# Starting the sums of x beside the last pieces of the attention's stage, with TensorE pinned to the source's order and two lent slots

## The chip, the cores and the metric

One core of a Trainium2 chip. The metric is the device time of one execution in microseconds; the kernel before takes 644.06 us (median of 3 runs, 642.32 to 644.40).

## What is computed

```python
# q, k, v: (2, 8, 768, 64) f32; sink of 4 keys, window of 128
a = softmax(where(is_sink | in_window, q @ k.T / 8, -1e9))
x = (a @ v) as 1536 rows of 512
x = ((x @ w_a) * (x @ w_b)) @ w_out            # 512 -> 1536 -> 512, first net
h = max(x @ moe2_w_in, 0)
out = (h * h) @ moe2_w_out                     # 512 -> 2048 -> 512, second net
```

Weights arrive in double precision, two 32-bit words a number.

## The kernel before

Every matmul is in single precision worked out of two rounded halves: a tile t becomes `hi` (a cast on ScalarE) and `lo = t - hi` (a subtraction on VectorE); the helper `split` does both (L66, L67). A product is then three matmuls: hi by hi, hi by lo, lo by hi. In the rows the halves of weights are `wh` and `wl`, those of x `xh` and `xl`, those of an intermediate g `gh` and `gl`. x is kept transposed in three blocks of 512 rows.

**Attention's stage.** A loop over 24 groups and three steps more (`attention_fast`), all engines in the source's order (`manual_schedule(engines=ORDERED)`). Beside it run *pieces* of the first net: of four columns blocks of w_a and w_b, for each of the three blocks of x, 12 matmuls into the PSUM tile `psa` (L657). There are 24 pieces, made by `Ffn.ahead`; `beside.asked` counts the pieces asked for in the loop. A piece of w_a is emptied by ScalarE into `u` (L670), the one of w_b by VectorE into `gs` (L674). `psa` has two buffers, so a piece waits for the emptying of the one two before it. The pieces of the third block need the last rows of x and so run after the loop, in `for at in beside.work` of `run`. There no engine's order is fixed: the planner of the framework orders what the source issues, by its own estimate of times. `ahead` yields None after each emptying; each such None calls `F.beat()`.

**Beats.** `beat` takes one step of a list of `chores` and lets `W.ahead()` convert one tile of weights every third beat (`PACE = 3`), if a slot (`W.free`) is there. A conversion of a weight tile (`Weights.stages`) is one ScalarE operation, four on VectorE (L534 to L541), a cast and a subtraction (L546, L548). `W.done` gives slots back when their weights are used up.

**The sums of x.** From phase 2 on, two blocks are multiplied by a scheme with seven products in place of eight (`unit`); it needs sums of the quarters of x in blocks 0 and 1. `first_sums` makes them in two halves (k = 0, 1), each in ten steps: four adds that put xh and xl together again into tiles `ks` (L704), two steps of two subtractions each (`sums_of`, L686 to L690), four splits, of which one overwrites block 1 of xh and xl. Each of these VectorE instructions is passed to `keep_in_program_order`, which puts it behind the instruction of its engine issued just before it in the source. So 20 steps in 20 beats.

**The second part** (`Ffn.run`), TensorE alone in the source's order. First the product with w_out of the eager columns: `one` for block 1, `two` for block 2, `held` for block 0, matmuls into `acc` (L916), each g split into gh and gl (3 buffers each, from a pool `wk` that is opened after the attention's pools have been closed), 6 matmuls for each half of g and a beat after each: 8, 8 and 4 beats. The first g is split into a lent slot of weights in place of gh and gl, so its matmuls read `wh` and `wl`. Then phase 2 with its first `unit` (px, py, pz, L786).

Of the kernel before, what the change touches and what calls it, by code (L numbers as in the profile page):

```python
# [21 lines left out]
AHEAD1 = 4  # L22
# [23 lines left out]
ET = mybir.EngineType  # L46
# [17 lines left out]
def split(nc, hi, lo, src, lo_eng=None):  # L64

    nc.scalar.copy(hi, src)  # L66
    return (lo_eng or nc.vector).tensor_sub(lo, src, hi.bitcast(F32))  # L67
# [571 lines left out]
class Ffn:  # L639
# [317 lines left out]
    def run(self, ps_y, ps_a, wk, keep):  # L957

        W = self.W
        self.ps_a, self.wk, self.keep = ps_a, wk, keep  # L960
        self.fresh, self.uses, self.fill, self.later, self.half = set(), {}, [], [], set()
        n1 = AHEAD1
        sizes = [len(p) for p in W.phases]

        def acc(ph, blk, ps, groups, final=0):
            return dict(net=ph >= W.second, blk=blk, ps=[], pool=(ps, "aaaa" if ps is ps_y else "xyzz"), total=3 * groups,
                        at=[0] * 4, final=final)

        def gs_of(blk):
            return [(1, f, self.gs[blk][:, f]) for f in range(n1)]  # L970

        one = acc(1, 1, ps_y, n1)
        slot = W.free.pop(0)
        split(self.tc.nc, *slot, gs_of(1)[0][2])
        self.chores.append(self.first_sums())
        yield from self.rest(one, gs_of(1), ready=[slot])
        W.free.append(slot)
        self.drain(one)
        two = acc(1, 2, ps_a, n1)
        yield from self.rest(two, gs_of(2))  # L980
        self.drain(two)
        held = acc(1, 0, ps_y, n1 + sizes[2])
        yield from self.rest(held, gs_of(0), 2)
        plan = {2: (0, 2, 1), 3: (1, 0, 2), W.second: (0, 1, 2)}
        for ph in range(W.second + 1, len(sizes)):
            a, b, c = plan[ph - 1]
            plan[ph] = (c, a, b)
        for ph in range(2, len(sizes)):
            now, mid, end = plan[ph]
            self.ph, self.now = ph, now  # L990
            self.kept = {mid: [], end: []}
            n, both = sizes[ph], ph < W.second
            lastly = ph in (W.second - 1, len(sizes) - 1)
            final = 2 - both if lastly else 0
            while self.chore():
                pass
            self.acc = held
            for key in self.later:
                self.queue(*key[:3], self.halves(key[3]))
            self.later = []  # L1000
            if ph == W.second:
                self.fill.append((self.drain, (held,)))
                self.acc = acc(ph, now, ps_y, n)
            self.acc["final"] = final
            late = LATE if both and lastly else 0
            step = 1 if both else 2
            other = acc(ph, mid, ps_a, n, final)
            lag, early = [], []

            def items(blk):  # L1010
                return [(ph, f, g) for f, g in sorted(self.kept[blk], key=lambda x: x[0])]

            def hook():
                if f + step == n:
                    early.append(self.halves(items(mid)[0][2]))

            for f in range(0, n, step):
                if f < n - late:
                    lag.append(f)
                woven = None  # L1020
                if lag and (lag[0] < f or ph != W.second):
                    woven = self.plain(ph, lag.pop(0))
                yield from self.unit(ph, f, woven, hook)
            for f in lag:
                for it in self.plain(ph, f):
                    yield from it
            while self.fill and not (both and now == 1 and len(self.fill) < 3) and len(self.fill) > 2 * (step - 1):
                self.more()
                yield
            yield from self.rest(other, items(mid)[:1], ready=early)  # L1030
            while self.fill:
                self.more()
                yield
            self.drain(self.acc)
            yield from self.rest(other, items(mid)[1:])
            self.drain(other)
            if not lastly:
                held = acc(ph, end, ps_y, n + sizes[ph + 1])
                yield from self.rest(held, items(end), 2)
                continue  # L1040
            held = acc(ph, end, ps_y, n, final)
            if both:
                self.chores.append(self.second_sums())
                self.pace = 2
                for f in range(n - late, n):
                    for it in self.plain(ph, f):
                        yield from it
                yield from self.rest(held, items(end), 2)
                continue
            yield from self.rest(held, items(end)[:-2])  # L1050
            its = items(end)[-2:]
            gs = [self.halves(g) for _, _, g in its]
            for d in range(4):
                for (p_, f, _), g in zip(its, gs):
                    self.outer(held, p_, f, g, 0, range(d, d + 1))
                self.drain(held, d)
            yield


@with_exitstack  # L1060
def sliding_window_moe_kernel(ctx, tc, q, k, v, vs, span, w_a, w_b, w_out, w_in2, w_out2, out):
    nc = tc.nc
    NT, DM = out.shape
    cp = ctx.enter_context(tc.tile_pool(name="cp", bufs=1))
    xp = ctx.enter_context(tc.tile_pool(name="xp", bufs=1))
    xh = xp.tile([P, DM // P, NT], F32R, name="xh")
    xl = xp.tile([P, DM // P, NT], F32R, name="xl")
    rp = ctx.enter_context(tc.tile_pool(name="rp", bufs=3))
    sa = ctx.enter_context(tc.tile_pool(name="sa", bufs=1))

    def slots(pool, n):
        return [(pool.tile([P, 512], F32R, name=f"wh{j}"), pool.tile([P, 512], F32R, name=f"wl{j}")) for j in range(n)]

    first = slots(sa, FIRST)
    zero = cp.tile([P, P], mybir.dt.bfloat16, name="zero")
    nc.vector.memset(zero, 0.0)
    mk = ctx.enter_context(ExitStack())
    tp = mk.enter_context(tc.tile_pool(name="mk", bufs=1, side="right"))
    c = setup(tc, cp, tp, span)

    def run(attend):
        W = Weights(tc, cp, rp, w_a, w_b, w_out, w_in2, w_out2)
        W.free = list(first)
        F = Ffn(tc, W, xh, xl, xp, out)
        with ExitStack() as c0:
            c0.callback(mk.close)
            wk0 = c0.enter_context(tc.tile_pool(name="wk0", bufs=2, side="right"))
            beside = Beside(tc, W, F, wk0, c0, zero, NT)
            with ExitStack() as c1, tc.manual_schedule(engines=ORDERED):
                attend(c1, beside)  # L1090
            with tc.tile_pool(name="sb", bufs=1) as sb, tc.tile_pool(name="ks", bufs=NKEEP) as keep:
                sx = slots(sb, NSUM)
                F.sx = {(n, k): sx[3 * k + n - 2] for n in range(2, 5) for k in range(2)}
                F.keep = keep
                for at in beside.work:
                    if at is None:
                        F.beat()
                c0.close()
                with ExitStack() as c2:
                    ps_y = c2.enter_context(tc.tile_pool(name="ps_y", bufs=4, space=PSUM))  # L1100
                    ps_a = c2.enter_context(tc.tile_pool(name="ps_a", bufs=1, space=PSUM))
                    wk = c2.enter_context(tc.tile_pool(name="wk", bufs=2))
                    c2.enter_context(tc.manual_schedule(engines={ET.PE}))
                    for _ in F.run(ps_y, ps_a, wk, keep):
                        F.beat()

    def attend_any(ctx, beside):
        attention_any(tc, c, q, k, v, xh, xl)
        beside.open()

    run(lambda ctx, beside: attention_fast(tc, ctx, c, cp, tp, q, k, v, vs, xh, xl, beside))
    slow = nc.values_load(c.slow[0:1, 0:1], min_val=0, max_val=1,
                          skip_runtime_bounds_check_because="the flag is 0 or 1")
    with tc.If(slow != 0):
        run(attend_any)
# [68 lines left out]
```

## Time and the profile before

| | |
|---|---|
| runs | 642.32, 644.06, 644.40 us; median 644.06 |
| profiled execution | 644.62 us |
| its span (first to last instruction) | 642.8 us |
| mean granted TensorE clock | 0.996 |
| TensorE busy | 621.2 us, 97% |
| VectorE busy | 483.1 us, 75% |
| ScalarE busy | 309.6 us, 48% |

The span is one execution on the chip, engine by engine: PE is TensorE's matmuls, DVE VectorE, ACT ScalarE. Times in the rows are microseconds from the span's start. A granted clock of 1.00 is TensorE's full clock.

### The profile page before, as it was taken

The page shows a single profiled execution, that of the slowest core. Times are in us where ns is not written, and L with a number is a line of the kernel's source. Part 1 is how long each engine was busy: PE and PEld are TensorE (multiplying, and loading weights), DVE is VectorE, ACT ScalarE, POOL GpSimd, SP SyncE. Part 2 cuts the span into 40 slices and gives each one's busy share as a digit, 9 for nine tenths or more (in the row PEclk, how much of TensorE's full clock was granted, in tenths as well). Part 3 has the DMA queues.
Part 4 walks back from the last instruction along what each step waited for, and adds up shares of the span by engine and source line. Part 5 has one row for each costly group of instructions (what it writes and reads, how often), then busy time and mean ns, then how long its engine had stood idle before and what let it go on. Part 6 is the DMA issues. An engine that isn't in the chain of part 4 may idle for free.

```text
span 642.8 us, 8846 instructions
## 1 busy us (share of the span) xinstructions
PE 621.2 (97%) x3110; PEld 498.0 (77%) x3110; DVE 483.1 (75%) x1094; ACT 309.6 (48%) x706; POOL 56.2 (9%) x132
## 2 busy tenths in 40 slices
PE   9889999998989999999999999999999999999996
PEld 6557777786767888888877787888887888888884
DVE  6989988246998867867858999986697769844352
ACT  6888777413664334523434645555435344322220
POOL 2564254300000000000000000000000000000000
PEclk9999999999998999999999999999999999999999
DMA  8634422012213230132212112232132112000023
GB/s 276 215 123 134 166 83 96 3 33 65 66 66 110 87 99 34 65 99 65 67 65 67 33 34 65 72 126 70 61 98 66 60 39 65 1 1 2 1 90 111
DMA packets 17413, 49.48 MB, mean 77 GB/s; under 512 B 2064, under 2 KB 2576, under 8 KB 17360
## 3 DMA queue, kind: packets, MB, share of 16 engines
q1 hardware_dynamic: 17216, 48.83, 23.4%
q8 instruction: 26, 0.43, 0.3%
q14 instruction: 27, 0.22, 0.1%
q10 hardware_dynamic: 144, 0.00, 0.0%
HBM read 45.68 MB, written 3.15 MB: 76 GB/s over the span
## 4 chain that ended last, share of the span: by engine, by line
PE 66%; DVE 8%; issue 1%; ACT 0%; DVEq 0%
PE acc L916 31%; PE psa L657 14%; PE px L786 12%; PE py L786 6%; PE pz L786 3%; DVE gl L67 1%; DVE wtmp L538 1%; DVE part L936 1%; DVE wtmp L534 1%; DVE wl L67 1%; DVE wtmp L541 1%; DVE wl L548 1%; DVE ks L704 0%; DVE xl L67 0%; ACT wtmp L530 0%
## 5 line engine op out<-in xcount | busy, mean ns | idle before, releaser
L657 PE MATMUL psa<-xh,wh 128*128 128x512 f32 x224 | 88.8, 396 | 0.5 <-DVE part L936 0.5
L657 PE MATMUL psa<-xh,wl 128*128 128x512 f32 x224 | 87.4, 390 | 0.0
L657 PE MATMUL psa<-xl,wh 128*128 128x512 f32 x224 | 87.2, 389 | 0.0
L916 PE MATMUL acc<-wh,gl 128*128 128x512 f32 x192 | 74.9, 390 | 1.1 <-DVE gl L67 1.1
L916 PE MATMUL acc<-wh,gh 128*128 128x512 f32 x192 | 74.7, 389 | 0.0
L916 PE MATMUL acc<-wl,gh 128*128 128x512 f32 x192 | 74.7, 389 | 0.0
L546 ACT CAST wh<-wtmp 128x512 fp32r<-128x512 f32 x68 | 42.3, 623 | 44.0 <-DVE wtmp L541 12.7
L548 DVE TENSOR_TENSOR wl<-wtmp,wh 128x512 fp32r<-128x512 f32 x68 | 47.4, 698 | 18.7 <-ACT wh L546 18.4
L916 PE MATMUL acc<-gl,wh 128*128 128x512 f32 x140 | 55.8, 399 | 2.8 <-DVE gl L67 2.8
L916 PE MATMUL acc<-gh,wh 128*128 128x512 f32 x140 | 55.3, 395 | 2.3 <-ACT gh L66 2.1
L66 ACT CAST gh<-ks 128x512 fp32r<-128x512 f32 x48 | 29.6, 621 | 55.6 <-PE acc L916 55.6
L916 PE MATMUL acc<-gh,wl 128*128 128x512 f32 x140 | 55.0, 393 | 0.0
L530 ACT ACTIVATE wtmp<-wraw 128x512 f32<-128x512 f32 x68 | 45.6, 673 | 17.4 <-DVE wl L67 12.0
L657 PEld LDWEIGHTS psa<-xh,wh 128*128 128x128 f32 x224 | 42.1, 188 | 9.1 <-DVE part L936 1.0
L657 PEld LDWEIGHTS psa<-xh,wl 128*128 128x128 f32 x224 | 42.0, 188 | 9.0
L657 PEld LDWEIGHTS psa<-xl,wh 128*128 128x128 f32 x224 | 42.1, 188 | 8.3
L538 DVE SCALAR_TENSOR_TENSOR wtmp<-wraw,wtmp 128x512 int32<-128x512 int32 x68 | 47.0, 695 | 0.5
L541 DVE SCALAR_TENSOR_TENSOR wtmp<-wraw,wtmp 128x512 int32<-128x512 int32 x68 | 46.4, 685 | 0.7
L916 PEld LDWEIGHTS acc<-wh,gl 128*128 128x128 f32 x192 | 36.0, 188 | 9.4 <-DVE gl L67 1.9
L534 DVE TENSOR_SCALAR wtmp<-wtmp 128x512 f32<-128x512 f32 x68 | 30.2, 445 | 16.9 <-ACT wtmp L530 16.2
L67 DVE TENSOR_TENSOR gl<-ks,gh 128x512 fp32r<-128x512 f32 x48 | 32.8, 686 | 12.4 <-ACT gh L66 12.0
L916 PEld LDWEIGHTS acc<-wh,gh 128*128 128x128 f32 x192 | 36.0, 188 | 7.5
(166 smaller groups left out, 1286.4 us busy)
## 6 DMA issues: line engine op xcount, KB each, us to landing
wraw<-in_moe_w_out_dram SPq DMA_DIRECT2D x28, 512.0 KB, 3.4
wraw<-in_moe_w_in_dram SPq DMA_DIRECT2D x16, 512.0 KB, 3.4
wraw<-in_moe_w_a_dram SPq DMA_DIRECT2D x12, 512.0 KB, 3.6
wraw<-in_moe_w_b_dram SPq DMA_DIRECT2D x12, 512.0 KB, 3.5
values<-in_v_dram SPq DMA_DIRECT2D x12, 256.0 KB, 4.0
out_dram<-part SPq DMA_DIRECT2D x12, 256.0 KB, 2.2
keys<-in_k_dram SPq DMA_DIRECT2D x11, 272.0 KB, 4.3
queries<-in_q_dram SPq DMA_DIRECT2D x11, 256.0 KB, 4.4
```

What stands on the lines that cost most here:

```text
L66: nc.scalar.copy(hi, src)
L67: return (lo_eng or nc.vector).tensor_sub(lo, src, hi.bitcast(F32))
L530: a = nc.scalar.activation(tf, up.bitcast(F32), AF.Abs)
L534: nc.vector.tensor_scalar(out=tf, in0=tf, scalar1=WMIN, scalar2=WMAX, op0=ALU.max, op1=ALU.min)
L538: nc.vector.scalar_tensor_tensor(out=t, in0=up, scalar=0x3FFFFFFF, in1=t, op0=ALU.bitwise_or, op1=ALU.bitwise_and)
L541: nc.vector.scalar_tensor_tensor(out=t, in0=low, scalar=29, in1=t, op0=ALU.logical_shift_right, op1=ALU.bitwise_or)
L546: nc.scalar.copy(hi, tf)
L548: nc.vector.tensor_sub(lo, tf, hi.bitcast(F32))
L657: self.tc.nc.tensor.matmul(ps, lhsT=w[:, kt, :], rhs=x[:, kt, ts], start=n == 0, stop=n == 3 * KT - 1)
L786: nc.tensor.matmul(ps, lhsT=a, rhs=b, start=start and k == 0 and j == 0, stop=k == 1 and j == 2, skip_group_check=True)
L916: nc.tensor.matmul(acc["ps"][d], lhsT=a, rhs=b, start=n == 0, stop=n == acc["total"] - 1)
L936: nc.vector.tensor_add(p_, p_, b_)
```

## The change

In `run`, the loop over the remaining pieces is put under the same pin of TensorE's order as the second part, and it starts `first_sums` as a chore at the first beat at which more than 16 pieces (`4 * AHEAD1`) are counted. `Ffn.run` no longer starts that chore, and it takes up to two slots in place of one for the halves of the first g tiles of `one`, and gives them back at the same place.

```diff
         one = acc(1, 1, ps_y, n1)
-        slot = W.free.pop(0)
-        split(self.tc.nc, *slot, gs_of(1)[0][2])
-        self.chores.append(self.first_sums())
-        yield from self.rest(one, gs_of(1), ready=[slot])
-        W.free.append(slot)
+        lent = [W.free.pop(0) for _ in range(min(2, len(W.free)))]
+        for slot, g in zip(lent, gs_of(1)):
+            split(self.tc.nc, *slot, g[2])
+        yield from self.rest(one, gs_of(1), ready=lent)
+        W.free += lent
         self.drain(one)
...
                 F.keep = keep
+                pieces, begun = beside.asked, False
+                c2 = ExitStack()
+                c2.enter_context(tc.manual_schedule(engines={ET.PE}))
                 for at in beside.work:
                     if at is None:
+                        pieces += 1
+                        if pieces > 4 * AHEAD1 and not begun:
+                            begun = True
+                            F.chores.append(F.first_sums())
                         F.beat()
                 c0.close()
-                with ExitStack() as c2:
+                with c2:
                     ps_y = c2.enter_context(tc.tile_pool(name="ps_y", bufs=4, space=PSUM))
                     ps_a = c2.enter_context(tc.tile_pool(name="ps_a", bufs=1, space=PSUM))
                     wk = c2.enter_context(tc.tile_pool(name="wk", bufs=2))
-                    c2.enter_context(tc.manual_schedule(engines={ET.PE}))
                     for _ in F.run(ps_y, ps_a, wk, keep):
                         F.beat()
```

## Rows read from the trace of the kernel before

**Rows 1.** The page, busy time, share of the span and instructions.

```profile
PE 621.2 (97%) x3110; PEld 498.0 (77%) x3110; DVE 483.1 (75%) x1094; ACT 309.6 (48%) x706; POOL 56.2 (9%) x132
```

**Rows 2.** Waits of TensorE: us in total, times, longest.

```profile
PE pst L318 <- POOL sp L288: 4.3, 6, 1.0
PE acc L916 <- DVE gl L67: 3.9, 8, 0.7
PE acc L916 <- ACT gh L66: 2.1, 1, 2.1
PE px L786 <- DVE wl L67: 1.6, 1, 1.6
PE px L786 <- ACT wh L66: 1.4, 1, 1.4
```

**Rows 3.** Busy time by stretch, with the granted clock (PEclk).

```profile
core 0: us, PE busy (x) PEld busy (x) DVE busy (x) ACT busy (x) POOL busy (x), PEclk, DMA share, GB/s
128.00:155.50 27.50, 27.50 (x124) 22.61 (x122) 11.73 (x22) 6.83 (x12) 0.00 (x0) 1.00 0.12 39
155.50:185.70 30.20, 25.94 (x109) 20.02 (x109) 30.17 (x56) 19.55 (x35) 0.00 (x0) 1.00 0.24 71
185.70:198.20 12.50, 9.49 (x34) 7.12 (x33) 12.09 (x26) 5.88 (x10) 0.00 (x0) 0.86 0.23 80
...
194.00:196.00 2.00, 1.83 (x5) 1.45 (x6) 2.00 (x6) 0.70 (x2) 0.00 (x0) 0.58 0.03 8
196.00:198.00 2.00, 2.00 (x7) 1.57 (x6) 2.00 (x4) 0.40 (x1) 0.00 (x0) 0.56 0.72 227
```

**Rows 4.** Timeline of TensorE, 139 to 186 us: start, duration, instruction, idle before.

```profile
139.18 0.39 PE L916 MATMUL acc<-wh,wh 128*128 128x512 f32 x1
...
147.11 0.39 PE L916 MATMUL acc<-wh,wl 128*128 128x512 f32 x1
...
155.27 0.39 PE L657 MATMUL psa<-xh,wl 128*128 128x512 f32 x1
157.79 0.49 PE L916 MATMUL acc<-gh,wh 128*128 128x512 f32 x1 [2.13 <-ACT gh L66]
158.83 0.50 PE L916 MATMUL acc<-gl,wh 128*128 128x512 f32 x1 [0.54 <-DVE gl L67]
...
185.73 0.39 PE L786 MATMUL px<-xh,wh 128*128 128x512 f32 x1
```

**Rows 5.** Timeline of TensorE in the first unit, 190 to 198 us.

```profile
190.27 0.39 PE L786 MATMUL px<-wh,wl 128*128 128x512 f32 x1
192.08 0.51 PE L786 MATMUL px<-wh,wh 128*128 128x512 f32 x1 [1.42 <-ACT wh L66]
194.17 0.67 PE L786 MATMUL px<-wl,wh 128*128 128x512 f32 x1 [1.59 <-DVE wl L67]
...
197.92 0.40 PE L786 MATMUL py<-xl,wh 128*128 128x512 f32 x1
```

**Rows 6.** Timeline of VectorE, 138 to 195 us.

```profile
138.50 1.29 DVE L704 TENSOR_TENSOR ks<-xh,xl 128x512 f32<-128x512 f32 x2
...
156.29 0.68 DVE L674 TENSOR_TENSOR gs<-u,psa 128x512 f32<-128x512 f32 x1
...
158.09 0.68 DVE L67 TENSOR_TENSOR gl<-gs,gh 128x512 fp32r<-128x512 f32 x1
158.69 0.68 DVE L704 TENSOR_TENSOR ks<-xh,xl 128x512 f32<-128x512 f32 x1
...
176.92 0.68 DVE L67 TENSOR_TENSOR gl<-gs,gh 128x512 fp32r<-128x512 f32 x1
...
193.43 0.68 DVE L67 TENSOR_TENSOR wl<-ks,wh 128x512 fp32r<-128x512 f32 x1
```

**Rows 7.** Timeline of ScalarE at the turn of the stages.

```profile
157.12 1.66 ACT L66 CAST gh<-gs 128x512 fp32r<-128x512 f32 x3 [2.38 <-issue]
```

## What the change was predicted to do

> **What bounds the kernel now.** The page comes first: TensorE is busy 97% of the span, VectorE 75% [rows 1]. So only two things can shorten the program: fewer matmuls, or less of the waiting that makes up the other 3%. The change removes no matmul. The list of TensorE's waits, read next, says where the waiting is: next to the transposes of the attention's stage, which the change does not touch, the large entries are `acc` waiting for the halves `gh` and `gl`, and `px` waiting for `wh` and `wl` [rows 2]. The timeline of TensorE places them. All the waits of `px` and the larger part of those of `acc` lie between 155 and 195 us, that is between the last pieces of the first two weight matrices and the first unit of phase 2. The table by stretch says who is late there: in 128 to 155.5 us VectorE is busy 11.73 of 27.5 us and TensorE never waits; in 155.5 to 185.7 us VectorE is busy 30.17 of 30.20 us and TensorE 25.94; in 185.7 to 198.2 us it is 12.09 and 9.49 of 12.5 us [rows 3]. An engine with 15.8 idle us stands right before a stretch in which the same engine is the bound. The change moves work from the second into the first.
>
> **Measure of a matmul.** From 139.18 to 155.27 us TensorE starts 72 matmuls without a break [rows 4], so one costs 16.09/71 = 0.227 us; the 0.39 us shown as duration overlaps the next. I count every loss as start to start less 0.227.
>
> **What the crowded stretch loses now.** After the last piece's last matmul (155.27) the next one starts at 157.79, and the one after it at 158.83 [rows 4]: 2.52 - 0.23 = 2.29 and 1.04 - 0.23 = 0.81, together 3.10 us. From 157.79 to the start of the first unit at 185.73 stand 108 matmuls, 24.48 us, but it took 27.94: 3.46 us lost, of which 0.81 is counted, so 2.65 us in three shorter waits for `gl` and the slower starts behind them. In the first unit, from 190.27 to 197.92 stand 11 intervals, 2.49 us, that took 7.65 [rows 5]: 5.15 us, of which 1.58 before 192.08, 1.86 before 194.17, and 1.71 behind that, where the granted clock is 0.58 and 0.56 [rows 3], so mostly the lower of its two levels (1.2 of 2.4 GHz). All of it: 3.10 + 2.65 + 5.15 = 10.9 us. This is the most that the change can win here.
>
> **TensorE in the source's order.** Now twelve matmuls of `acc` (those fed by the one lent slot) run among the pieces, the first at 139.18, the last at 147.11 [rows 4]. Pinned, they follow the pieces. TensorE is gapless there either way, so the order alone costs nothing; the pieces end 12 x 0.227 = 2.72 us earlier, their last matmul starting at 152.55.
>
> **Two slots lent.** Why does TensorE wait at 155.5? ScalarE casts the first `gh` at 157.12 [rows 7], right after VectorE has emptied the last piece (156.29, for 0.68 us) [rows 6]; until then it did nothing. The tiles gh and gl come from a pool opened after the old one is closed, so I read it as waiting for that space. The lent slots lie elsewhere. With two of them 24 matmuls are ready at 152.78 and run to 158.22. From the last piece's start to the end of the first gl it took 158.77 - 155.27 = 3.50 us [rows 4, 6]; the same chain now gives 156.05, 2.2 us before it is wanted. So the 3.10 us go as a whole. The cover costs one more subtraction on VectorE and one cast on ScalarE, the second done by about 141 us (that slot's weights are last read by the third piece after the loop, over near 139), in VectorE's idle time. If that cover failed, VectorE would owe 0.60 us. The free slots left for the weights are one fewer for eight beats; I followed the list through the beats: the six conversions of those 20 beats all find their slots in the same beats as before. No DMA is added, and SP's loads keep their places between the conversions.
>
> **The sums begin with the pieces.** At the loop's end 16 pieces are asked, so the condition (over 16) holds at the first of the nine beats that are left. Nine steps of the twenty then run in these beats: four adds, four subtractions of the first half, three splits. That is 11 instructions of VectorE, each 0.60 us start to start (158.09 to 158.69) [rows 6]. Two of the adds already stand at 138.50; the third split is behind the last piece's emptying and stays at the edge. So 8 x 0.60 = 4.8 us leave the crowded stretch, with the lent slot's split 5.4 us, and go into 15.8 idle us. ScalarE's casts move with them; it is busy 19.55 of 30.2 us in the crowded stretch and less before [rows 3].
>
> What does that give? First the unit. Its second product waits for the sums' second half: the `wl` made from `ks` at 193.43 [rows 6], over at 194.11, wanted at 190.50, so 3.6 us late. Its step moves from beat 17 to beat 8 of the second part, 9 beats of 6 matmuls, 12.2 us of TensorE's program; TensorE itself comes 5.75 us earlier at the most. 12.2 - 5.75 - 3.6 leaves 2.8 us to spare: both waits go, and the low clock behind them with them. I take the whole 5.15; bounds 0 (the step is as late as before) and 5.15. Second the gl waits. The last late gl is at 176.92 [rows 6]. Ahead of it go 7 steps of the sums and one gl, 8 x 0.60 = 4.8, and the stretch begins 2.7 us earlier: 169.4. But the second half's subtractions and splits now stand ahead of it in the source, up to 8 x 0.60 = 4.8 more: 174.2. It is wanted at 152.78 + 14 x 1.36 = 171.8. So it comes between 2.4 us early and 2.4 us late. I take half of the 2.65 as won, 1.3, bounds 0 and 2.65.
>
> **The queue that the steps enter.** A step is pinned behind the VectorE instruction traced before it, so no step overtakes an emptying of PSUM, but once in the queue it stands before the next one, and TensorE needs that bank two pieces on. A piece takes 12 x 0.227 = 2.72 us; the emptying takes 0.68; so some 2.0 us may stand before it at no cost. The longest step is two subtractions, 1.2 us. I put it at nothing; the cover is those 2 us, and what exceeds them TensorE pays in full. The Trainium skill ("PSUM — Partial Sum Buffer", Engine vs sequencer instructions) calls VectorE's queue strictly first in, first out. By that rule a split that waits for its cast holds the emptying behind it too, and the sum would lose what exceeds the 2 us at each of four emptyings (the slower case below). The trace agrees as far as it goes: the gl of 176.92 came late in a stretch where VectorE was never idle [rows 3, 6].
>
> **Sum.** 3.10 + 1.3 + 5.15 = 9.5 us. The profiled execution took 644.62 us with a span of 642.8 (1.8 around it): 633.3 span, 635.1 us. The median of the runs is 644.06, 0.56 below, so 634.6 us.
>
> **Rivals.**
> *The late sums stay.* The pins hold the steps behind the emptyings of the pieces and the conversions, or conversions fill VectorE's new room: the unit's wait remains or moves to the weights' own sums. For it: VectorE owes over 30 us of work by the unit. Against: the 12.2 us of program order. Gain 3.10 + 1.3: 639.7 us.
> *The change does not do what it says.* The steps run where they ran and VectorE's new order makes as many waits in later phases as the turn gains. In its favour, VectorE's and ScalarE's other instructions are ordered anew by a planner that does not know the chip's real times, and waits of 0.3 to 0.7 us stand in later phases already (8 waits for gl in all [rows 2]). Gain 0 to 2: about 643.
> *Slower.* Steps that wait for their casts stand before the four emptyings on VectorE that follow, and TensorE, pinned, has nothing else to run. To eat 9.5 us and pass the 0.3% bound (1.9 us) takes 11.4 us, 2.9 at each, so a queue of 4.9 us before each. From 2.0 it costs, from 4.4 (9.5/4 + 2.0) it decides. Such a case would give 646 or more. Against it: VectorE sits idle over half of that stretch.
> *All of it.* The gl waits go too: 644.06 - 10.9 = 633.2.
>
> **Numbers.** Forecast 0.58 (own range 632.5 to 637); all of it 0.12; late sums stay 0.14; no change 0.08; slower 0.08. The range runs from 632, one us under the most, to 640.5, just past the case of the late sums; about 2 in 10 lie outside. What a measurement of this kernel can tell from no change is 0.3%, 1.9 us. Faster 0.85 (three cases and a little of the fourth), same 0.07, slower 0.08.
>
> **What would show it.** Right: no matmul of `acc` among the pieces, the last piece over at about 153; no wait of `acc` for `gh`; the add-and-subtract steps on ks between 131 and 150; the first unit at 180 to 181.5; no wait of px, clock 1.00 throughout; VectorE under 95% in the 30 us before the unit. Wrong: waits of psa for the emptied u or gs among the pieces (slower), px still waiting for wl near 184 to 188 (late sums), or new waits behind 200 us that add up to more than 2 us.

## The result and the profile after

The changed kernel takes 633.35 us (median of 4 runs, 633.00 to 633.96) against 644.23 for the kernel before beside it; the ratio is 0.9835, 95% interval 0.981 to 0.986. That is 10.9 us less. The profiled execution has a span of 631.6 us, 11.2 less. The forecast was 634.6, in a range of 632 to 640.5.

Three places are named as in the prediction: the turn is the stretch right behind the last piece's last matmul, the gl waits are the three shorter waits from there to the first unit, and the unit is the first unit of phase 2.

TensorE's waits in the changed kernel (us in total, times, longest); they answer to [rows 2]:

```profile
PE pst L318 <- POOL sp L288: 4.5, 6, 1.0
PE acc L916 <- DVE gl L67: 1.8, 4, 0.7
...
PE psa L657 <- DVE part L936: 0.5, 1, 0.5
```

No wait of `px` is left, none of `acc` for gh, and four of the eight for gl are gone; the four that stay lie behind 300 us and are as they were. The stretches of [rows 3] in the changed kernel, and the 30 us ahead of its first unit:

```profile
128.00:155.50 27.50, 27.50 (x123) 22.75 (x123) 21.28 (x38) 10.42 (x19) 0.00 (x0) 1.00 0.12 39
155.50:185.70 30.20, 30.20 (x135) 25.02 (x134) 28.28 (x55) 19.32 (x36) 0.00 (x0) 1.00 0.27 88
185.70:198.20 12.50, 12.50 (x56) 10.35 (x56) 12.46 (x26) 6.45 (x12) 0.00 (x0) 1.00 0.39 126
149.60:179.60 30.00, 30.00 (x134) 24.86 (x133) 29.23 (x54) 18.95 (x34) 0.00 (x0) 1.00 0.25 80
```

In each line the stretch, its length and TensorE's busy time are followed by the busy time of the weight loads and of VectorE: 21.28 us of the first stretch are in use on VectorE now, 11.73 before. Up to the end of the pieces, at 152.44 us, it is 18.22 of 24.44. TensorE is busy without a break and at its full clock. Its timeline at the places of [rows 4] and [rows 5]:

```profile
146.77 0.39 PE L657 MATMUL psa<-xh,wl 128*128 128x512 f32 x1
...
152.21 0.39 PE L657 MATMUL psa<-xh,wl 128*128 128x512 f32 x1
152.44 0.39 PE L916 MATMUL acc<-wh,wh 128*128 128x512 f32 x1
...
157.65 0.39 PE L916 MATMUL acc<-wh,wl 128*128 128x512 f32 x1
157.88 0.39 PE L916 MATMUL acc<-gh,wh 128*128 128x512 f32 x1
158.10 0.39 PE L916 MATMUL acc<-gl,wh 128*128 128x512 f32 x1
...
171.71 0.39 PE L916 MATMUL acc<-gl,wh 128*128 128x512 f32 x1
...
179.64 0.39 PE L786 MATMUL px<-xh,wh 128*128 128x512 f32 x1
...
184.40 0.39 PE L786 MATMUL px<-wh,wh 128*128 128x512 f32 x1
...
314.95 0.50 PE L916 MATMUL acc<-gl,wh 128*128 128x512 f32 x1 [0.28 <-DVE gl L67]
```

Two lines of the kernel before, from VectorE's and from TensorE's timeline, that these places are compared with:

```profile
128.83 0.42 DVE L348 TENSOR_TENSOR xl<-x,xh 128x256 fp32r<-128x256 f32 x1 [4.20 <-ACT xh L345]
...
326.21 0.50 PE L916 MATMUL acc<-gl,wh 128*128 128x512 f32 x1 [0.28 <-DVE gl L67]
```

The first unit starts at 179.64, 6.09 us before the 185.73 of [rows 4]. Of these 0.34 come from the attention's stage, which starts a little earlier in this execution (its last `xl` is at 128.49 here and at 128.83 before); 5.75 are the turn and the gl waits. The next wait behind is at 314.95 here and was at 326.21: 11.26 earlier, so the first unit gives 5.17. Behind it nothing changes. VectorE's timeline, which answers to [rows 6]:

```profile
128.49 0.42 DVE L348 TENSOR_TENSOR xl<-x,xh 128x256 fp32r<-128x256 f32 x1 [4.20 <-ACT xh L345]
130.88 0.69 DVE L674 TENSOR_TENSOR gs<-u,psa 128x512 f32<-128x512 f32 x1 [1.97 <-PE psa L657]
131.48 1.29 DVE L704 TENSOR_TENSOR ks<-xh,xl 128x512 f32<-128x512 f32 x2
...
141.83 0.69 DVE L674 TENSOR_TENSOR gs<-u,psa 128x512 f32<-128x512 f32 x1 [1.00 <-PE psa L657]
...
144.60 0.69 DVE L690 TENSOR_TENSOR ks<-ks 128x512 f32<-128x512 f32 x1
...
148.13 0.68 DVE L674 TENSOR_TENSOR gs<-u,psa 128x512 f32<-128x512 f32 x1
...
153.87 0.69 DVE L674 TENSOR_TENSOR gs<-u,psa 128x512 f32<-128x512 f32 x1
...
156.28 1.30 DVE L67 TENSOR_TENSOR gl<-gs,gh 128x512 fp32r<-128x512 f32 x2
...
166.46 0.69 DVE L686 TENSOR_TENSOR ks<-ks 128x512 f32<-128x512 f32 x1
...
168.60 0.69 DVE L67 TENSOR_TENSOR gl<-gs,gh 128x512 fp32r<-128x512 f32 x1
...
172.28 0.69 DVE L689 TENSOR_TENSOR ks<-ks 128x512 f32<-128x512 f32 x1
...
176.23 0.69 DVE L67 TENSOR_TENSOR wl<-ks,wh 128x512 fp32r<-128x512 f32 x1
```

The adds and subtractions of the first half run from 131.48 to 145.29, and none of them holds up an emptying (`gs`). The half that the unit's second product needs (`wl` at 176.23, the lower half of what L689 made at 172.28) is over at 176.92, and the matmuls that need it begin at 184.40. The chain that ended last names VectorE nowhere in this stretch:

```profile
128.04 24.56 PE psa L657 x108
152.60 27.20 PE acc L916 x120
179.80 1.36 PE px L786 x6
181.16 1.36 PE pz L786 x6
```

Before, it ran on VectorE from 154.21 to 177.66:

```profile
154.21 0.44 DVE wtmp L534
...
177.00 0.62 DVE gl L67
177.66 8.24 PE acc L916 x35
```

### The profile page after: what moved, and what is told of

Same layout as the page of the kernel before. It is cut to its first block, busy times and chain, and to the rows that moved or that the text cites. A ratio compares the mean times of both kernels' runs of the same rounds, so it can differ in the third digit from the quotient of the medians.

```text
span 631.6 us, 8848 instructions
## 1 busy us (share of the span) xinstructions
PE 616.6 (98%) x3110; PEld 497.1 (79%) x3110; DVE 483.2 (77%) x1094; ACT 309.3 (49%) x706; POOL 56.2 (9%) x132
## 4 chain that ended last, share of the span: by engine, by line
PE 90%; DVE 7%; ACT 1%; issue 1%; POOL 0%; POOLq 0%; DVEq 0%; ACTq 0%
PE acc L916 34%; PE psa L657 24%; PE px L786 13%; PE py L786 6%; PE pz L786 3%; PE x L332 3%; PE sc L233 3%; PE ptp L294 1%; PE x L337 1%; DVE ex L249 1%; ACT ex L257 1%; DVE part L936 1%; DVE wtmp L538 1%; DVE gl L67 1%; DVE wtmp L541 1%
## 5 line engine op out<-in xcount | busy, mean ns | idle before, releaser
L916 PE MATMUL acc<-gl,wh 128*128 128x512 f32 x136 | 53.3, 392 | 0.7 <-DVE gl L67 0.7
L916 PE MATMUL acc<-gh,wh 128*128 128x512 f32 x136 | 53.1, 391 | 0.2
L916 PE MATMUL acc<-gh,wl 128*128 128x512 f32 x136 | 52.9, 389 | 0.0
L538 DVE SCALAR_TENSOR_TENSOR wtmp<-wraw,wtmp 128x512 int32<-128x512 int32 x68 | 47.2, 699 | 0.5
L916 PEld LDWEIGHTS acc<-wl,gh 128*128 128x128 f32 x192 | 36.0, 188 | 7.5
```

Source lines behind the costliest of these rows:

```text
L538: nc.vector.scalar_tensor_tensor(out=t, in0=up, scalar=0x3FFFFFFF, in1=t, op0=ALU.bitwise_or, op1=ALU.bitwise_and)
L916: nc.tensor.matmul(acc["ps"][d], lhsT=a, rhs=b, start=n == 0, stop=n == acc["total"] - 1)
```

## The experiments

**The parts alone and in pairs.** The change has three parts: two slots, the pin of TensorE beside the pieces, the early sums. Six kernels carry the other combinations. The parts that are undone, against the changed kernel:

```diff
-        lent = [W.free.pop(0) for _ in range(min(2, len(W.free)))]
+        lent = [W.free.pop(0) for _ in range(min(1, len(W.free)))]   # one slot
...
-                c2.enter_context(tc.manual_schedule(engines={ET.PE}))  # no pin: entered
                 for at in beside.work:                                 # behind the pieces
...
-                            F.chores.append(F.first_sums())  # late sums: the chore starts
+                            pass                             # in Ffn.run, as before
```

Two slots alone: 

> Two slots alone; TensorE unpinned beside the pieces, the sums start late as in the kernel before. Theory A (the slots only help if TensorE keeps the lent matmuls for the turn): the planner runs nearly all 24 lent matmuls among the pieces, the last piece ends about 2.7 us later, and the wait for gh behind it stays at about 2 us; px waits for the late sums as before. Gain 0 to 1 us, about 643.5. Rival B (the second slot is itself the cover of the turn): the 3.1 us at the turn go, about 641.

Early sums alone: 

> The early sums alone; one slot, TensorE unpinned beside the pieces. Theory A (three separate losses, of which the early sums pay for the unit's wait and low clock, 5.15 us, and for most of the late gl, 2.65): no wait of px, clock 1.00, but the turn's wait of about 2 us for gh stays. Gain 5 to 8 us, about 637.5. Rival B (the early sums alone free VectorE enough that the turn's wait shrinks too): gain 9 or more, under 635.

The pin alone: 

> The pin of TensorE beside the pieces alone; one slot, late sums. Theory A: the twelve lent matmuls now lie behind the last piece and cover 2.7 of the 3.5 us that gh and gl take; the turn loses 0.8 in place of 3.1 us, the unit's waits for the late sums stay. Gain 2.3 us, about 642. Rival B (the pin without more to run costs as much as it covers): about 644.

Pin and slots: 

> Pin and two slots, late sums. Theory A: the turn's 3.1 us go whole, some of the late gl too; the unit's waits for px stay between 3 and 5 us, as VectorE still makes all late sums in the crowded stretch and TensorE only comes earlier. Gain 3 to 5 us, about 640. Rival B (a shorter turn gives VectorE its time back and the unit's waits shrink as well): under 637.

Pin and early sums: 

> The change with one slot in place of two: pin and early sums. Theory A (the second slot is worth what one slot leaves open at the turn): twelve lent matmuls cover 2.7 of 3.5 us, so TensorE waits under 1 us for gh or gl at the turn, all else as in the changed kernel. About 634.2, 0.8 above the change. Rival B (both slots are needed, the wait for gh comes back whole): 636 or more.

Early sums and slots: 

> The change without the pin beside the pieces: early sums and two slots. Theory A (without the pin the lent matmuls are spent among the pieces): the turn's wait for gh of 2 us or more is back, no wait of px. About 636.3, some 3 above the change. Rival B (the pin is needless once VectorE is free): 633.5.

Measured, with the start of the first unit and the waits of TensorE from each one's profile (a ratio is against runs of the kernel before on the same chip, whose median was 644.50 us beside the kernels slots, sums, pin and pin, slots, and 642.84 beside pin, sums and sums, slots; the change was compared with the 644.23 of the first line, and small differences between rows are to be read from the ratios):

| kernel | median us | ratio to before, 95% interval | unit starts | waits at the turn (gh, gl) | waits in the unit (px) |
|---|---|---|---|---|---|
| before | 644.23 | 1 | 185.73 | 2.13, 0.54 | 1.42, 1.59 |
| slots | 646.41 | 1.0028 (1.0019 to 1.0038) | 183.41 | 1.68, 0.54 | 4.18, 2.06 |
| pin | 642.23 | 0.9968 (0.9956 to 0.9980) | 179.96 | 0, 0.22 | 3.75, 1.90 |
| sums | 639.75 | 0.9924 (0.9911 to 0.9938) | 185.75 | 2.49, 1.20 | none |
| pin, slots | 639.63 | 0.9924 (0.9910 to 0.9937) | 179.83 | none | 1.94, 1.39 |
| pin, sums | 635.66 | 0.9882 (0.9858 to 0.9906) | 182.0 | 0, 1.20 | none |
| sums, slots | 637.03 | 0.9907 (0.9886 to 0.9928) | 184.0 | 1.49, 0.94 | none |
| all three | 633.35 | 0.9835 (0.9810 to 0.9860) | 179.64 | none | none |

Three things follow. First, the pin is what makes the slots a cover: without it the planner starts all 24 lent matmuls before the last piece is over, and the turn's wait stays (slots; sums and slots). Second, the early sums end the unit's waits in every combination that has them, and no combination without them ends these. Third, the losses do not add up. The pin alone brings the unit forward by 5.8 us, yet the kernel gains 2.3: the unit waits 5.65 us instead of 3.01. The slots alone bring it forward by 2.3 us and the kernel becomes 1.9 us slower. The rows of the pin alone show it, with matmuls at the lower clock behind the waits (granted clock 0.50 in 192 to 194 us):

```profile
179.96 0.39 PE L786 MATMUL px<-xh,wh 128*128 128x512 f32 x1
...
188.63 0.79 PE L786 MATMUL px<-wh,wh 128*128 128x512 f32 x1 [3.75 <-ACT wh L66]
191.32 0.80 PE L786 MATMUL px<-wl,wh 128*128 128x512 f32 x1 [1.90 <-DVE wl L67]
191.92 0.63 PE L786 MATMUL px<-wh,wl 128*128 128x512 f32 x1
```

For the slots alone the expectation of a gain of up to 1 us was wrong in sign. The early sums alone gain 4.75 us, a little under the 5 to 8 expected: the turn's waits are longer than before there and the clock falls behind them (last section), so the unit starts no earlier. Pin and early sums were expected at 634.2 and came at 635.66: with one slot the wait for gl is 1.20 us. The timeline of VectorE there says why:

```profile
154.36 0.68 DVE L674 TENSOR_TENSOR gs<-u,psa 128x512 f32<-128x512 f32 x1
154.96 0.69 DVE L67 TENSOR_TENSOR wl<-ks,wh 128x512 fp32r<-128x512 f32 x1
155.56 1.29 DVE L541 SCALAR_TENSOR_TENSOR wtmp<-wraw,wtmp 128x512 int32<-128x512 int32 x2
156.76 0.69 DVE L67 TENSOR_TENSOR gl<-gs,gh 128x512 fp32r<-128x512 f32 x1
```

A split and two steps of conversions stand between the emptying and gl. The chain from the last piece to the end of gl is 4.76 us in this run too (152.69 to 157.45), and twelve lent matmuls cover 2.72 of it.

**Where gh waits at the turn.** One slot, pin and early sums, but gh and gl in a pool opened before the pieces:

```diff
-        gh = self.wk.tile([P, T], F32R, name="gh", tag="gh", bufs=3)
+        gh = self.hk.tile([P, T], F32R, name="gh", tag="gh", bufs=3)   # gl alike
...
+                F.hk = c2.enter_context(tc.tile_pool(name="hk", bufs=2))
                 for at in beside.work:
```

> Pin, early sums and one slot (2.3 us above the change, with a wait for gl of 1.2 us at the turn), but gh and gl lie in a pool of their own, opened before the last pieces. Theory A (at the turn gh and gl wait for the space of the closed pool, which the last emptying sets free): gh is cast before the last emptying, no wait at the turn, and the time of the change with two slots, 633.3. Rival B (VectorE's queue alone makes gl late there): still 635 or more.

It takes 633.63 us (0.9843, 0.9822 to 0.9863), the time of the change, and TensorE has no wait at the turn. ScalarE casts the first gh before the last emptyings:

```profile
128.33 1.14 ACT L66 CAST gh<-gs 128x512 fp32r<-128x512 f32 x2
131.58 0.62 ACT L66 CAST gh<-gs 128x512 fp32r<-128x512 f32 x1 [2.11 <-DVE gs L674]
```

So gh did wait for the space of the closed pool, and a pool of its own is worth what the second slot is.

**The turn alone.** The same pool in the kernel before, nothing else.

> The kernel before with gh and gl in a pool of their own, opened before the last pieces; one slot, no pin, late sums. Theory A (VectorE's work in the crowded stretch is the bound, so what the turn wins is in part waited again for the late sums): the turn's wait goes, the unit's waits grow from 3.0 to 4 us or more; gain 1 to 3.5 us, 641 to 643.5. Rival B (the losses add up): the whole 3.1 to 5.7 us of the turn, under 640.

644.64 us, ratio 1.0007 (0.9993 to 1.0021): nothing gained, less than the 1 to 3.5 us expected. The unit starts at 180.13, 5.6 us earlier, and then:

```profile
191.02 0.80 PE L786 MATMUL px<-wh,wh 128*128 128x512 f32 x1 [5.96 <-ACT wh L66]
192.98 0.68 DVE L67 TENSOR_TENSOR wl<-ks,wh 128x512 fp32r<-128x512 f32 x1
193.71 0.79 PE L786 MATMUL px<-wl,wh 128*128 128x512 f32 x1 [1.90 <-DVE wl L67]
...
185.70:200.00 14.30, 7.08 (x20) 5.33 (x21) 14.06 (x28) 6.63 (x11) 0.00 (x0) 0.64 0.31 93
```

The `wl` that it waits for starts at 192.98, against 193.43 in [rows 6]: VectorE finishes about when it did, though TensorE comes 5.6 us earlier. The last line is the busy time of the stretch: VectorE 14.06 of 14.30 us, the granted clock 0.64.

**How early the sums must start.** The chore begins at the fifth of the nine beats:

```diff
-                        if pieces > 4 * AHEAD1 and not begun:
+                        if pieces > 5 * AHEAD1 and not begun:
```

> The change with the sums begun four beats later (at the fifth of nine beats): five steps early in place of nine. In the changed kernel the sums that the unit's second product needs are over 7 us before they are wanted; four beats are 5.4 us. Theory A (the early start is worth its place only until the sums are in time): no wait of px, 633.3 to 634.3. Rival B (each step moved is worth its share of VectorE's time, 4/9 of 7.8 us): 636 to 637.

637.16 us (635.13 to 637.83; ratio 0.9906, 0.9885 to 0.9927); the reading by beats was wrong. The wait is back:

```profile
186.56 0.50 PE L786 MATMUL px<-wl,wh 128*128 128x512 f32 x1 [1.89 <-DVE wl L67]
```

Its `wl` starts at 185.82, 9.6 us later than the 176.23 of the change, for four beats that are 5.4 us of TensorE. The beats that were left out lie in VectorE's idle time (from 128 us to the end of the pieces it is busy 12.98 of 24.30 us here, 18.22 of 24.44 in the change); their work moves into the full stretch and takes other work's place there. The profiled execution took 635.51 us, near the lower end of the six; four of the others took 637.03 to 637.83, and where these lose 2 us more no trace shows.

**Twice as many.** `F.chore()` is called once more before `F.beat()` beside the pieces, so 18 of the 20 steps start there.

> The change with two steps of the sums a beat beside the pieces, so 18 of 20 steps start there. The forecast's slower case names a queue of steps before the emptyings of PSUM, with some 2 us to spare. Theory A (the spare holds, and nothing is left to win in the crowded stretch): 633.3, within 0.5 of the change, no wait of psa. Rival B (more steps in the queue hold the emptyings and TensorE, pinned, waits): waits of psa for u or gs, 2 us or more above the change.

633.08 us (0.9849, 0.9824 to 0.9873), no wait of psa for an emptied u or gs, the unit without a wait. VectorE is busy 23.43 of the 27.5 us from 128 on. The queue before the emptyings costs nothing even so.

**Less to do in place of earlier.** Pin and two slots with late sums, and weights converted every fourth beat until phase 2:

```diff
-        if self.beat >= PACE and self.convert():
+        if self.beat >= self.pace and self.convert():   # PACE + 1, PACE from phase 2 on
```

> Pin and two slots with late sums (waits of px 1.9 and 1.4 us), but until phase 2 weights are converted every fourth beat in place of every third, so some two conversions of about 2.5 us of VectorE fewer stand before the unit. Theory A (how much VectorE has to do before the unit sets the waits, not the place of the sums as such): the waits of px shrink by more than half; 635 to 638 against 639.6. Rival B (the sums' late place in the source sets them): 639 or more.

634.04 us (0.9852, 0.9831 to 0.9872) against 639.63 for the same kernel at the old pace; 635 to 638 was expected. One wait of px is left, 0.39 us; its `wl` starts at 184.50, against 187.84 at the old pace. From 128 to 184.4 us VectorE has run the first two-operand step of a conversion (L538, here one line further down) 6 times instead of 7, so one conversion less, not two, and that one is missing before 152.3 us, where VectorE has idle time. From 152.3 us to that `wl` seven other instructions are missing, one set of sums of weights above all (L560 to L563 and a split), some 3 us: as much as the `wl` comes earlier. The sums stand as late in the source as before the change: it is the amount of VectorE's work in the full stretch ahead of the unit that makes them late.

**The waits that are left.** Two steps a beat, and a higher priority for every split into gh and gl.

```diff
-        split(self.tc.nc, gh, gl, g)
+        with self.tc.high_priority(offset=60):
+            split(self.tc.nc, gh, gl, g)
```

> The change, two steps of the sums a beat beside the pieces, and every split into gh and gl with a higher priority for the planner, against the five short waits that are left behind 300 us (2.3 us in all, some 3 with the slower starts). Theory A (gl comes behind conversions only because the planner sees no hurry): most of these waits go, 630.5 to 632. Rival B (the hurried halves push conversions and emptyings back): 633 or more.

633.40 us (0.984, 0.982 to 0.9861): no gain, where 630.5 to 632 was hoped for. The four waits for gl and the one of psa are there with the same lengths, 0.28 to 0.66 us. At the longest, gl still stands behind a PSUM addition and a conversion's step, so the priority did not change VectorE's order there. What would is open. No version tried beats the changed kernel by more than the runs scatter.

## Why the prediction was right

**What bounds the kernel.** Right, and the experiments make it sharper: between 150 and 195 us the bound is VectorE's work ahead of the unit's sums, and the change gains by filling VectorE's idle time before. VectorE was forecast under 95% in the 30 us ahead of the unit; it is 29.23 of 30.00, 97%. It stays nearly full; only TensorE no longer waits for it. The unit was forecast to start at 180 to 181.5 and starts at 179.64.

**The turn, 3.10 us.** Taken whole, as forecast. The pieces' last matmul starts at 152.21, or 152.55 on the clock of the kernel before, the figure forecast. The chain from there to the end of gl was mis-sized: 3.50 us forecast, 4.76 measured (152.21 to 156.97), as steps of other work stand in between. The cover, 24 matmuls, holds 1.1 us over that (158.10). A cover of one slot does not, as the run with one slot shows.

**The gl waits, 1.3 of 2.65 us.** The term that was mis-sized: all 2.65 us went (5.75 for turn and gl together). I let gl come between 2.4 us early and 2.4 us late; it came at the early end. The split that was last to be late before (176.92) is the one at 168.60 here, over at 169.29 and read at 171.71. Of the eight subtractions and splits of the sums' second half that I let stand ahead of it, one does (L686 at 166.46).

**The unit, 5.15 us.** Right: 5.17. The reason was too simple. The step was said to have 2.8 us to spare, from beats; it has 7.5 (176.92 to 184.40). The run that starts four beats later shows that beats do not measure it: its step came 9.6 us later, not 5.4.

**The order and the queue at nothing.** Right, with room: twice the steps cost nothing either. Two emptyings start late, with steps of conversions in front of them: the one at 148.13 comes 1.36 us after its piece's last matmul (146.77) and the last one, at 153.87, comes 1.66 us after its own (152.21), where the one at 141.83 comes 0.50 us after its own (141.33). TensorE waits for neither. The Trainium skill ("PSUM — Partial Sum Buffer", Engine vs sequencer instructions) has VectorE's queue strictly first in, first out. The trace agrees in that these two emptyings and gl come behind steps of conversions; a split of the sums that holds up an emptying no run here shows.

**The sum.** 9.5 forecast, 10.9 measured; "all of it" was the case that came, at 10.9. The sum treated its terms as separate. They are not: pin and slots, which clear the turn, are worth 6.4 us when the sums are in time (639.75 to 633.35; by the ratios 5.7), and clearing the turn alone is worth about nothing (644.64). The rival of the late sums, put at 639.7, is the pair of pin and slots, which took 639.63. That the numbers meet is in part luck: the pair gains 4.9 us on a median of 644.50, where 4.4 on 644.06 was said, as the gl waits go whole and the unit loses a little more than before.

## What to carry to other kernels

When two waits follow each other in one stretch and the same engine is behind both, removing the first only moves its time into the second; count that engine's work up to the last date that matters, and move or drop work until it is done in time. Matmuls that are ready early are a cover for a wait only if the order keeps them for it; a planner that fills idle-looking places spends them. And a tile that waits for the space of a pool just closed can be freed by opening its pool earlier, if there is room.

## What the runs showed of the hardware

The granted clock fell behind some pairs of waits with one matmul between them, and not behind others. In the kernel before it is 0.58 and 0.56 after waits of 1.42 and 1.59 us [rows 3, 5], but stays 1.00 behind 2.13 and 0.54 us at the turn. With early sums and slots it is 0.50 in 162 to 164 us, behind 1.49 and 0.94 us. A wait without a second one near it left the clock at 1.00 at 1.20 us (pin and early sums) and at 1.89 us (the later start), while in the one of 5.96 us (the turn alone) it was at 0.50 before TensorE started again. What decides between these cases no run here shows. With the early sums alone it falls at the turn, behind 2.49 and 1.20 us: matmuls then start every 0.43 us, nearly twice the usual 0.227, so it is the lower level, 1.2 GHz of 2.4.

```profile
158.06 0.50 PE L916 MATMUL acc<-gh,wh 128*128 128x512 f32 x1 [2.49 <-ACT gh L66]
159.77 0.64 PE L916 MATMUL acc<-gl,wh 128*128 128x512 f32 x1 [1.20 <-DVE gl L67]
160.21 0.63 PE L916 MATMUL acc<-gh,wl 128*128 128x512 f32 x1
160.63 0.63 PE L916 MATMUL acc<-gh,wh 128*128 128x512 f32 x1
```

On one chip the mean clock and the time of the kernel before go together: of 11 runs, those with a mean clock of 0.989 took 643.98 to 645.64 us and those with 0.995 to 0.997 took 641.88 to 642.87. The 17 runs on a second chip go the same way (0.989 and 0.990: 644.27 to 646.05; 0.996 and 0.997: 642.24 to 642.87). On a third they do not: 15 runs with 0.989 to 0.996 took 643.65 to 645.33 us in no such order. The four runs of the changed kernel, which has no wait left at the turn or in the unit, have 0.997 or 0.998 and took 633.00 to 633.96. That it scatters less because the waits are gone is likely, but not shown.

The Trainium skill ("TensorE: Matmul & The Clock Gate", What's actually happening) says that the throttled clock is the default and activity releases it. The trace of the kernel before agrees with the second half: behind the two waits of the unit TensorE is busy without a break, and the clock is 0.56 in 196 to 198 us [rows 3] and 1.00 in 198 to 200. That the lower level is the default no run here shows.
